# The gate's logits computed with the tokens stationary and the gate's weights moving

## The chip, the cores and the metric

The kernel runs on one core of a Trainium2 chip. The core has a matrix engine (TensorE; PE in the profile, with its weight loads shown apart as PEld), VectorE (DVE), ScalarE (ACT), GpSimd (POOL) and the DMA queues, which SyncE (SP) starts. The metric is the device time of one execution in microseconds (us), as the median of several runs.

A matrix multiplication on TensorE is a pair of instructions. A weight load (LDWEIGHTS) puts the *stationary* operand into the array, at most 128 columns of it, and a MATMUL then streams the *moving* operand past it. The output has the stationary operand's columns on its partitions and the moving operand's columns along its rows.

## What is computed

Three stages follow one another: an attention with packed keys, a dense layer with a clipped activation, and a mixture of eight experts. The change is in the third stage's first line:

```python
logits = x @ w_gate                  # x: 2304 x 512, w_gate: 512 x 8
logits = logits - logits.max()
P = np.exp(logits)
for _ in range(8):
    P /= P.sum(1, keepdims=True) + 1e-09
    P /= P.sum(0, keepdims=True) + 1e-09
    P *= N / E
for e in range(E):                   # E = 8 experts
    h = np.maximum(x @ w1[e], 0.0)
    out += P[:, e:e + 1] * (h @ w2[e])
```

## The kernel before

The 2304 tokens are cut into six blocks of 384. While the dense layer is computed, its result `x` is summed in `acc[blk]`, one tile for a block: the 512 features lie on 128 partitions in four chunks (KC = 4), and the block's 384 tokens lie along the rows. The dense layer's first product is `layer1a` (lines 871 to 873 of the code), its second `layer2a` (lines 908 to 910), whose result VectorE adds into `acc` (line 929). Each of these products is made of three MATMULs, since numbers are split into a high and a low part. The expert stage does the same with `layer1b` (lines 982 to 984) and `layer2b` (lines 1040 to 1042); `operands` (from line 941) prepares what `layer1b` multiplies.

`gate(blk)` makes the logits of one block, and there are six such calls. Before the change a gate has four steps:

1. Line 1100: four matmuls, one for each chunk of 128 features. The chunk of `wg` is stationary, padded from 8 to 32 columns with zeros, and the chunk of 384 tokens moves. Each writes another 32 of the 128 output partitions (a column tile), so the four lie side by side in the array, and what comes out are four partial sums. The operands are plain float32, and the profile shows two pairs of instructions for one such matmul.
2. `copy` (line 297 on ScalarE, 298 on VectorE): the 128x384 partial sums go from PSUM to a tile `tmp`.
3. Line 1110: three transposes of 128x128 put the tokens on the partitions.
4. Line 1117: VectorE adds the four partial sums and writes 24 numbers on each partition into `L`.

When `L` is whole, `routing()` finds the largest logit and does the eight rounds of normalizing, on VectorE, with two small matmuls for the maximum (lines 1131 and 1140) and one in each round for the sum over the tokens (line 1170: a 128x128 tile of ones is stationary, 8 columns move).

The order of the instructions is made by a planner in the kernel (`Order.run`): every step has an engine, a cost in us that the author wrote down, a priority and the tiles it needs, and the planner puts next whatever can start first by these costs. So an edit to one step's cost or tiles can change the order of its neighbours on every engine. The planner only sets the order; on the chip each engine takes its instructions in that order and waits where an operand isn't there. The gate has priority 41 and runs as soon as its block of `acc` is finished, among the products of the dense layer; its steps stand at 0.75 us and 0.36 us on TensorE in the plan.

Of the kernel before, what the change touches and what calls it, by code (L numbers as in the profile page):

```python
# [12 lines left out]
ALU = mybir.AluOpType  # L13
AX = mybir.AxisListType
# [119 lines left out]
def t_dve(n, fast=False):  # L134
    return 0.065 + n / (1920.0 if fast else 960.0)


def t_act(n, psum=False):
    return (0.05 if psum else 0.095) + n / 1200.0
# [11 lines left out]
def tile_kernel(  # L151
# [16 lines left out]
    nc = tc.nc  # L168
# [4 lines left out]
    E, _, F2 = moe2_w1.shape  # L173
    KC = DM // 128
# [5 lines left out]
    TB = 384  # L180
# [7 lines left out]
    def pool(name, stack=ctx, **kw):  # L188
        return stack.enter_context(tc.tile_pool(name=name, bufs=1, **kw))

    const, dp, accp, hp, wp = (pool(n) for n in ("const", "dp", "accp", "hp", "wp"))
    ph = pool("ph", space=PSUM)
# [7 lines left out]
    def place(tag, where, count, late=0):  # L200

        res[tag] = Res(count)
        res[tag].pool, res[tag].first, res[tag].late = where, count, late
# [49 lines left out]
    ident = const.tile([128, 128], F32, name="ident")  # L253
# [17 lines left out]
    def hold(tag, shape, dt=F32):  # L271
        return Hold(res[tag], maker(tag, shape, dt, ("",)))
# [5 lines left out]
    def pe(cost, fn, **kw):  # L278
        return order.op([("PE", cost, fn)], **kw)

    def dve(cost, fn, **kw):
        return order.op([("DVE", cost, fn)], **kw)
# [4 lines left out]
    def gps(cost, fn, **kw):  # L287
        return order.op([("POOL", cost, fn)], **kw)
# [4 lines left out]
    def copy(dst, src, n, **kw):  # L293

        return order.op(
            [
                ("ACT", t_act(n, True), lambda: nc.scalar.activation(dst(), src(), AF.Copy)),  # L297
                ("DVE", t_dve(n), lambda: nc.vector.tensor_copy(dst(), src()), EASE),
            ],
            **kw,  # L300
        )
# [88 lines left out]
    def whole(g, which, prio, tag, early=False):  # L390

        _, w1, w2, f0 = groups[g]
        if which == "w1":
            src = w1[:, f0:f0 + FG].rearrange("(c p) f -> p c f", p=128)
        else:
            src = w2[f0:f0 + FG, :].rearrange("(c p) d -> p c d", p=128)
        wide = src.dtype == I64
        shape = list(src.shape)
        w = hold(tag, shape) if which == "w1" else pair(tag, shape)
        per = shape[1] // (2 if wide else 1)  # L400
        for i in range(0, shape[1], per):
            r = raw_piece(src[:, i:i + per, :], prio, turn_of("raw", early))

            def at(t, i=i, c0=0, n=per * shape[2]):
                return t[:, i:i + per, :].rearrange("p c n -> p (c n)")[:, c0:c0 + n]

            if wide:
                n = DEC_EARLY if early else DEC
                for c0 in range(0, per * shape[2], n):
                    split_f64(  # L410
                        r, c0, n, w, lambda t, at=at, c0=c0, n=n: at(t, c0=c0, n=n), prio, which == "w2",
                        "m_early" if early else "m",
                    )
            else:
                split_part(at, lambda r=r: r.t, w, per * shape[2], [r], prio)
        return w
# [396 lines left out]
    acc = [hold(f"acc{j}", [128, KC, TB]) for j in range(NB)]  # L813
# [3 lines left out]
    def psum(tag):  # L817
        return hold(tag, [128, 512])

    def tmp():  # L820
        return hold("tmp", [128, TB])
# [261 lines left out]
    def once(name, shape, dt=F32):  # L1083
        if name not in res:
            place(name, None, 0, 1)
        return hold(name, shape, dt)

    Pr = once("Pr", [128, NTT, E])
    L = once("L", [128, NTT * E])
    wg = once("wg", [128, KC, 32])  # L1090

    def gate(blk):
        c0 = blocks[blk][0] // 128
        nt = TB // 128
        kw = dict(prio=41)
        ps, lg = psum("ph"), tmp()

        def mm():
            for c in range(KC):
                nc.tensor.matmul(  # L1100
                    ps.t[32 * c:32 * c + 32, :TB], wg.t[:, c, :], acc[blk].t[:, c, :], start=True, stop=True
                )

        pe(0.75, mm, reads=[acc[blk], wg], writes=[ps], **kw)
        copy(lambda: lg.t, lambda: ps.t[:, :TB], TB, reads=[ps], writes=[lg], **kw)
        pt = psum("ph")

        def trans():
            for t in range(nt):
                nc.tensor.transpose(  # L1110
                    pt.t[:, t * 128:(t + 1) * 128], lg.t[:, t * 128:(t + 1) * 128], ident
                )

        pe(0.12 * nt, trans, reads=[lg], writes=[pt], **kw)
        dve(
            t_dve(nt * E * KC),
            lambda: nc.vector.tensor_reduce(
                L.t[:, c0 * E:(c0 + nt) * E].rearrange("p (t e) -> p t e", e=E),
                pt.t[:, :nt * 128].rearrange("p (t c e) -> p t e c", t=nt, c=KC)[:, :, :E, :],
                AX.X, ALU.add,  # L1120
            ),
            reads=[pt], fills=[L], **kw,
        )

    def routing():
# [68 lines left out]
    def early(gg):  # L1194

        return (9.4, 9.4, 13.4, 14.4, 100, 100, 100, 100)[gg]

    with tc.manual_schedule():
        nc.vector.memset(ones, 1.0)
        nc.vector.memset(three, 3.0)  # L1200
        nc.vector.memset(maskb, 0.0)
        nc.vector.memset(maskb[0:64, 0, :], 1.0)
        nc.vector.memset(maskb[64:128, 1, :], 1.0)
        nc.vector.memset(maskz, 0.0)
        for g in range(2):
            for h in range(2):
                r0 = 64 * g + 32 * h
                nc.vector.memset(maskz[r0:r0 + 32, g, h, :], 1.0)

        place("p0", att, 1)  # L1210
        place("p1", att, 1)
        p_sb = hold("p0", [128, 1, D]), hold("p1", [128, NU - 1, D])
        for u in range(NU):
            attention(u, p_sb)
        ws, pws = {}, {}

        def weights(gg):
            prio, soon = early(gg), gg < 4
            ws[gg] = (
                whole(gg, "w1", prio, "w1f", soon),  # L1220
                whole(gg, "w2", prio + 0.5, ("w2", "w2o")[gg % 2], soon),
            )

        for gg in range(4):
            weights(gg)
        order.op([("", 0.0, second_phase)], after=order.all)

        gps(0.2, lambda: nc.gpsimd.memset(wg.t, 0.0), writes=[wg], prio=90)
        dma(
            16,  # L1230
            lambda: nc.sync.dma_start(wg.t[:, :, :E], moe2_w_gate.rearrange("(c p) e -> p c e", p=128)),
            writes=[wg], prio=90,
        )
        begun = len(order.all)
        for i, (b, g, half) in enumerate(units):
            for gg in (2 * g, 2 * g + 1):
                if gg not in ws:
                    weights(gg)
                if (b, gg) not in pws:
                    pws[b, gg] = packed_weights(i, b, ws[gg][0])  # L1240
            hs = [pair("hs", [128, NFC, TB]) for _ in range(2)]
            for f in range(2 * NFC):
                layer1a(i, b, half, f, pws[b, 2 * g + f // NFC], hs[f // NFC])
            layer2a(i, g, b, half, [ws[2 * g][1], ws[2 * g + 1][1]], hs)
        uses = [[o for o in order.all[begun:] if a2[b] in o.holds] for b in range(B)]
        freed = []
        for b, count in enumerate((1, 2, 1, 2)):
            freed = [order.op([("", 0.0, first_operands(count))], after=[*uses[b], *freed])]
        order.op([("", 0.0, third_phase)], after=order.all[begun:])
        for blk in range(NB):  # L1250
            gate(blk)
        ops = {0: operands(0, 40)}
        routing()
        i = len(units)
        turn, done = 100 + G1, []
        for ps in passes:
            for pr in ps:
                if pr not in ops:
                    ops[pr] = operands(pr, 45 if pr > 1 else 200, [done[-1] if pr > 1 else done[6]])
            for g in range(G1, len(groups)):  # L1260
                wa, wb = combined(g, turn)
                w2 = whole(g, "w2", turn, "w2")
                turn += 1
                for pr in ps:
                    hs = [pair("hs", [128, NFC, TB]) for _ in range(2)]
                    done.append(layer1b(i, ops[pr], wa, wb, hs))
                    for h in range(2):
                        layer2b(i, g, 2 * pr + h, w2, hs[h])
                    i += 1
        order.run()  # L1270
# [32 lines left out]
```

## Time and profile before

| | |
|---|---|
| three runs | 1964.9, 1965.55 and 1965.96 us; median 1965.55 us |
| the profiled execution's own time | 1963.38 us |
| its span, first to last instruction | 1961.6 us |
| TensorE busy | 1918.5 us, 98% of the span |
| VectorE, ScalarE, GpSimd busy | 62%, 50%, 46% |
| share of TensorE in the chain that ended last | 87% |
| mean granted TensorE clock | 0.996 |

The profile shows one execution. A line of the timeline gives the start, the length, the engine, the code's line, output and inputs, and in brackets how long the engine had stood idle and for whom. MATMULs overlap: a new one starts before the listed end of the last, so what an instruction costs TensorE is read from start to start, and the listed ends are modelled. The granted clock is 1.00 at 2.4 GHz and 0.50 at 1.2 GHz.

### The profile page before, as it was taken

The numbers are of one execution on the slowest core, as the hardware profiler recorded it, in microseconds if no ns is written. First come the engines' busy times: TensorE is split into PE (matmuls) and PEld (weight loads), VectorE is DVE, ScalarE is ACT, GpSimd is POOL, SyncE is SP. The second block draws the span as 40 slices with busy tenths as digits, with TensorE's granted clock in tenths as the row PEclk, the third lists the DMA queues.
The fourth block names the chain that finished last, engine by engine and source line by source line (L and its number), as shares of the span: only waits on it lengthen the run. The fifth ranks groups of instructions, "written<-read, shape, count | busy, mean of one in ns | idle before, by whom it ended". The sixth has DMA issues, their size and how long they took to land.

```text
span 1961.6 us, 29114 instructions
## 1 busy us (share of the span) xinstructions
PE 1918.5 (98%) x10957; PEld 1733.8 (88%) x10957; DVE 1213.5 (62%) x2110; ACT 981.4 (50%) x2273; POOL 897.4 (46%) x961
## 2 busy tenths in 40 slices
PE   6899999999999999999999999999999999999998
PEld 4789989988989999999889999999999999999997
DVE  6886687446876666666736655555555555555554
ACT  6885775445465555554553444434444343444432
POOL 2454576346665555555633434334243333434321
PEclk9999999999999999999999999999999999999999
DMA  9920121001212222222311101011110110101002
GB/s 211 202 79 27 53 68 50 12 1 44 65 54 76 65 66 74 65 65 75 87 33 33 33 33 44 22 43 33 33 44 22 44 33 33 42 24 44 29 15 65
DMA packets 103549, 104.92 MB, mean 53 GB/s; under 512 B 42736, under 2 KB 78576, under 8 KB 103408
## 3 DMA queue, kind: packets, MB, share of 16 engines
q1 hardware_dynamic: 103408, 103.06, 19.2%
q8 instruction: 86, 1.41, 0.3%
q14 instruction: 55, 0.45, 0.1%
HBM read 98.32 MB, written 4.72 MB: 53 GB/s over the span
## 4 chain that ended last, share of the span: by engine, by line
PE 87%; DVE 5%; ACT 2%; POOL 2%; DMA 2%; issue 1%; SPq 0%; POOLq 0%; ACTq 0%; DVEq 0%
PE po L1042 13%; PE po L1040 13%; PE po L1041 13%; PE ph L982 12%; PE ph L984 12%; PE ph L983 12%; PE po L908 2%; PE po L909 2%; PE po L910 2%; PE ph L871 1%; POOL m L341 1%; DMA raw<-in_moe_w_out_dram 1%; PE ph L873 1%; PE ph L872 1%; PE ph L833 1%
## 5 line engine op out<-in xcount | busy, mean ns | idle before, releaser
L426 POOL TENSOR_TENSOR hsl<-tmp,hsh 128x384 fp32r<-128x384 f32 (+1 forms) x418 | 402.8, 975 | 815.9 <-PE ph L984 483.6
L1064 DVE SCALAR_TENSOR_TENSOR acc<-po,Pr,acc 128x512 f32<-128x512 f32 x504 | 372.8, 747 | 288.0 <-PE po L1042 286.5
L1042 PE MATMUL po<-w2h,hsl 128*128 128x512 f32 x1152 | 449.0, 390 | 0.4 <-DVE hsl L426 0.4
L1040 PE MATMUL po<-w2h,hsh 128*128 128x512 f32 x1152 | 449.1, 390 | 0.0
L1041 PE MATMUL po<-w2l,hsh 128*128 128x512 f32 x1152 | 449.0, 390 | 0.0
L297 ACT ACTIVATE tmp<-ph 128x384 f32<-128x384 f32 x291 | 141.2, 485 | 411.9 <-PE ph L984 405.6
L996 DVE TENSOR_TENSOR tmp<-ph,tmp 128x384 f32<-128x384 f32 x288 | 159.1, 552 | 267.1 <-PE ph L984 189.4
L1042 PEld LDWEIGHTS po<-w2h,hsl 128*128 128x128 f32 x1152 | 216.3, 188 | 45.8 <-DVE hsl L426 0.8
L1040 PEld LDWEIGHTS po<-w2h,hsh 128*128 128x128 f32 x1152 | 216.5, 188 | 41.5
L1041 PEld LDWEIGHTS po<-w2l,hsh 128*128 128x128 f32 x1152 | 216.4, 188 | 41.3
L421 ACT ACTIVATE hsh<-tmp 128x384 fp32r<-128x384 f32 (+1 forms) x512 | 245.5, 498 | 13.1 <-DVE tmp L886 8.9
L421 ACT ACTIVATE w2h<-raw 128x1024 fp32r<-128x1024 f32 x64 | 68.0, 1063 | 326.5 <-PE po L1042 318.1
L982 PE MATMUL ph<-ax,w1h 128*128 128x384 f32 x512 | 173.1, 338 | 0.6 <-ACT tmp L297 0.6
L983 PE MATMUL ph<-ax,w1h 128*128 128x384 f32 x512 | 172.6, 337 | 0.0
L984 PE MATMUL ph<-ax,w1l 128*128 128x384 f32 x512 | 172.5, 337 | 0.0
L1004 ACT ACTIVATE tmp<-tmp 128x384 f32<-128x384 f32 x288 | 149.7, 520 | 31.2 <-DVE tmp L996 24.8
L426 POOL TENSOR_TENSOR w1l<-raw,w1h 128x256 fp32r<-128x256 f32 (+1 forms) x123 | 155.8, 1267 | 0.0
L982 PE MATMUL ph<-xyh,w1xh 128*128 128x384 f32 x320 | 108.4, 339 | 0.1
L984 PE MATMUL ph<-xyh,w1xl 128*128 128x384 f32 x320 | 108.0, 337 | 0.0
L983 PE MATMUL ph<-xyl,w1xh 128*128 128x384 f32 x320 | 107.8, 337 | 0.0
L881 ACT ACTIVATE tmp<-ph,three 128x288 f32<-128x288 f32 x128 | 63.1, 495 | 85.1 <-PE ph L873 84.1
L426 POOL TENSOR_TENSOR w1xl<-m,w1xh 128x256 fp32r<-128x256 f32 x130 | 105.1, 827 | 0.2
(206 smaller groups left out, 4038.7 us busy)
## 6 DMA issues: line engine op xcount, KB each, us to landing
raw<-in_moe_w_dram SPq DMA_DIRECT2D x128, 512.0 KB, 3.6
raw<-in_moe_w_in_dram SPq DMA_DIRECT2D x16, 512.0 KB, 3.9
raw<-in_moe_w_out_dram SPq DMA_DIRECT2D x16, 512.0 KB, 3.8
k<-in_k_dram SPq DMA_DIRECT2D x32, 144.0 KB, 5.7
q<-in_q_dram SPq DMA_DIRECT2D x32, 144.0 KB, 4.8
v<-in_v_dram SPq DMA_DIRECT2D x8, 576.0 KB, 6.8
out_dram<-acc SPq DMA_DIRECT2D x36, 128.0 KB, 2.3
p<-in_p_dram SPq DMA_DIRECT2D x1, 224.0 KB, 5.5
```

The lines of the kernel that those rows point to most:

```text
L297: ("ACT", t_act(n, True), lambda: nc.scalar.activation(dst(), src(), AF.Copy)),
L421: t_act(n), lambda: nc.scalar.activation(dst(w.t[0]), src(), AF.Copy),
L426: lambda e: e.tensor_tensor(dst(w.t[1]), src(), as_f32(dst(w.t[0])), ALU.subtract),
L982: nc.tensor.matmul(out, wh[:, at + c, :], bh[:, c, :], start=first and c == 0, **on)
L983: nc.tensor.matmul(out, wh[:, at + c, :], bl[:, c, :], start=False, **on)
L984: nc.tensor.matmul(out, wl[:, at + c, :], bh[:, c, :], start=False, **on)
L996: t_dve(n), lambda: nc.vector.tensor_tensor(u.t, ps.t[:, :n], u.t, ALU.add),
L1004: t_act(n, bool(ps)), lambda: nc.scalar.activation(c.t, src(), AF.Relu),
L1040: nc.tensor.matmul(ps.t, hh[:, f, ts], wh[:, f, :], start=(f == 0), stop=False)
L1041: nc.tensor.matmul(ps.t, hh[:, f, ts], wl[:, f, :], start=False, stop=False)
L1042: nc.tensor.matmul(ps.t, hl[:, f, ts], wh[:, f, :], start=False, stop=(f == NFC - 1))
L1064: lambda row=row, share=share, ps=ps: nc.vector.scalar_tensor_tensor(row(), ps.t, share(), row(), ALU.mult, ALU.add),
```

## The change

The two operands of the gate's matmuls change places. A block's tokens are now stationary, 128 tokens at a time, and the eight columns of the gate's weights move past them. A block has three groups of 128 tokens and four chunks of features, so there are twelve matmuls where four were, and the chunks are summed in PSUM (`start` on the first, `stop` on the last). The result has the tokens on the partitions already. ScalarE's copy, the three transposes and VectorE's sum over the four parts go; VectorE copies 24 numbers on each partition into `L`. `wg` is no longer padded, and GpSimd's memset of it goes. The gate's one step on TensorE stands at 1.6 us in the plan.

```diff
-    wg = once("wg", [128, KC, 32])
+    wg = once("wg", [128, KC, E])
...
-        kw = dict(prio=41)
-        ps, lg = psum("ph"), tmp()
+        ps = psum("ph")
 
         def mm():
-            for c in range(KC):
-                nc.tensor.matmul(
-                    ps.t[32 * c:32 * c + 32, :TB], wg.t[:, c, :], acc[blk].t[:, c, :], start=True, stop=True
-                )
-
-        pe(0.75, mm, reads=[acc[blk], wg], writes=[ps], **kw)
-        copy(lambda: lg.t, lambda: ps.t[:, :TB], TB, reads=[ps], writes=[lg], **kw)
-        pt = psum("ph")
-
-        def trans():
             for t in range(nt):
-                nc.tensor.transpose(
-                    pt.t[:, t * 128:(t + 1) * 128], lg.t[:, t * 128:(t + 1) * 128], ident
-                )
-
-        pe(0.12 * nt, trans, reads=[lg], writes=[pt], **kw)
+                for c in range(KC):
+                    nc.tensor.matmul(
+                        ps.t[:, t * E:(t + 1) * E], acc[blk].t[:, c, t * 128:(t + 1) * 128], wg.t[:, c, :],
+                        start=(c == 0), stop=(c == KC - 1),
+                    )
+
+        pe(1.6, mm, reads=[acc[blk], wg], writes=[ps], prio=41)
         dve(
-            t_dve(nt * E * KC),
-            lambda: nc.vector.tensor_reduce(
-                L.t[:, c0 * E:(c0 + nt) * E].rearrange("p (t e) -> p t e", e=E),
-                pt.t[:, :nt * 128].rearrange("p (t c e) -> p t e c", t=nt, c=KC)[:, :, :E, :],
-                AX.X, ALU.add,
-            ),
-            reads=[pt], fills=[L], **kw,
+            t_dve(nt * E),
+            lambda: nc.vector.tensor_copy(L.t[:, c0 * E:(c0 + nt) * E], ps.t[:, :nt * E]),
+            reads=[ps], fills=[L], prio=41,
         )
...
-        gps(0.2, lambda: nc.gpsimd.memset(wg.t, 0.0), writes=[wg], prio=90)
         dma(
             16,
-            lambda: nc.sync.dma_start(wg.t[:, :, :E], moe2_w_gate.rearrange("(c p) e -> p c e", p=128)),
+            lambda: nc.sync.dma_start(wg.t, moe2_w_gate.rearrange("(c p) e -> p c e", p=128)),
             writes=[wg], prio=90,
         )
```

The planner's order around it moves too. On TensorE at the first gate, where `layer1a` (lines 871 to 873) runs on both sides of it, the order before is (a line has the code's line, the operation, output and inputs, the output's size, and a count; the numbers count tiles):

```order
L873 MATMUL ph_5345<-ax_94,pwl_5146 128x288
L1100 MATMUL ph_5356<-acc_0_1253,wg_2229 32x384 x4
L871 MATMUL ph_5366<-ax_94,pwh_5145 128x288
L872 MATMUL ph_5366<-ax_94,pwh_5145 128x288
L873 MATMUL ph_5366<-ax_94,pwl_5146 128x288
L871 MATMUL ph_5366<-ax_94,pwh_5145 128x288
L872 MATMUL ph_5366<-ax_94,pwh_5145 128x288
L873 MATMUL ph_5366<-ax_94,pwl_5146 128x288
L1110 MATMUL ph_5376<-ident,tmp_5373 128x128 x3
```

and now, on the same engine at the same place:

```order
L873 MATMUL ph_5344<-ax_94,pwl_5145 128x288
L1100 MATMUL ph_5355<-wg_2229,acc_0_1253 128x8 x12
L871 MATMUL ph_5374<-ax_94,pwh_5144 128x288
L872 MATMUL ph_5374<-ax_94,pwh_5144 128x288
L873 MATMUL ph_5374<-ax_94,pwl_5145 128x288
L871 MATMUL ph_5374<-ax_94,pwh_5144 128x288
L872 MATMUL ph_5374<-ax_94,pwh_5144 128x288
L873 MATMUL ph_5374<-ax_94,pwl_5145 128x288
```

The gate is one piece in the same place, and the three transposes behind the next six MATMULs are gone; the other five gates change in the same way.

On VectorE, at the last gate and the entry of the routing (`w2l` and `w1l` are the low parts of the experts' weights; line 996 adds parts of `layer1b`; lines 1129 and 1134 take the maximum, 1143 copies it), the order before is:

```order
L959 TENSOR_TENSOR tmp_6147<-acc_0_1253,acc_0_1607 128x384
L426 TENSOR_TENSOR w2l_6141<-raw_4614,w2h_6140 128x1024
L1117 TENSOR_REDUCE L_5392<-ph_6184 128x24
L1129 TENSOR_REDUCE mx_6199<-L_5392 128x1
L996 TENSOR_TENSOR tmp_6160<-ph_6190,tmp_6160 128x384
L426 TENSOR_TENSOR w1l_6210<-raw_5128,w1h_6209 128x512
L996 TENSOR_TENSOR tmp_6182<-ph_6201,tmp_6182 128x384
L1134 TENSOR_REDUCE mm_6229<-ph_6216 1x1
L996 TENSOR_TENSOR tmp_6085<-ph_6190,tmp_6085 128x384
L1143 COPY nm_6259<-ph_6248 128x1
```

and now (lines 1108, 1116, 1121 and 1130 are the copy into `L`, the two maxima and the copy of the maximum):

```order
L959 TENSOR_TENSOR tmp_6165<-acc_0_1253,acc_0_1607 128x384
L426 TENSOR_TENSOR w2l_6159<-raw_4613,w2h_6158 128x1024
L1108 COPY L_5382<-ph_6171 128x24
L1116 TENSOR_REDUCE mx_6200<-L_5382 128x1
L1121 TENSOR_REDUCE mm_6213<-ph_6202 1x1
L996 TENSOR_TENSOR tmp_6106<-ph_6204,tmp_6106 128x384
L1130 COPY nm_6230<-ph_6216 128x1
L426 TENSOR_TENSOR w1l_6228<-raw_5127,w1h_6227 128x512
```

The three steps that lead to the maximum stand closer together: one addition of line 996 is left between them, where three and a split of weights stood. On TensorE the two small matmuls of the maximum come that much earlier too: six MATMULs of `layer1b` lie between the last gate and the first of them, and six between the first and the second.

## Rows read from the trace of the kernel before

**Rows 1.** The page: busy time of each engine, and the last chain's shares.

```profile
PE 1918.5 (98%) x10957; PEld 1733.8 (88%) x10957; DVE 1213.5 (62%) x2110; ACT 981.4 (50%) x2273; POOL 897.4 (46%) x961
PE 87%; DVE 5%; ACT 2%; POOL 2%; DMA 2%; issue 1%; SPq 0%; POOLq 0%; ACTq 0%; DVEq 0%
```

**Rows 2.** Stretches: PE, PEld, DVE, ACT, POOL busy; PE clock, DMA share, GB/s.

```profile
130.00:380.00 250.00, 244.35 (x1795) 225.10 (x1793) 166.86 (x378) 153.24 (x400) 139.60 (x174) 1.00 0.16 47
380.00:465.00 85.00, 83.98 (x619) 76.54 (x618) 38.59 (x93) 37.22 (x85) 37.73 (x42) 1.00 0.03 7
```

**Rows 3.** Timeline at the first gate: start us, length us, engine, line, operation.

```profile
388.00 0.29 PE L873 MATMUL ph<-ax,pwl 128*128 128x288 f32 x1
388.22 0.16 PEld L1100 LDWEIGHTS ph<-acc,wg 128*32 128x32 f32 x8 [0.16 <-DVE acc L929]
...
389.24 0.29 PE L872 MATMUL ph<-ax,pwh 128*128 128x288 f32 x1
...
389.28 0.49 ACT L297 ACTIVATE tmp<-ph 128x384 f32<-128x384 f32 x1 [0.39 <-PE ph L1100]
...
389.77 0.30 PE L873 MATMUL ph<-ax,pwl 128*128 128x288 f32 x1
...
389.90 0.49 PE L1110 MATMUL ph<-ident,tmp 128*128 128x128 f32 x3
...
390.36 0.29 PE L872 MATMUL ph<-ax,pwh 128*128 128x288 f32 x1
```

**Rows 4.** Line 1100 of all gates: what its weight loads waited for, us, times.

```profile
  DVE acc L929: 0.8, 5
```

**Rows 5.** Line 1170, the routing's sum over tokens: weight loads, ns min/median/max.

```profile
L1170 PEld LDWEIGHTS ph<-cs,ones x16: 186/188/192, 471.2 to 511.6; 128*128 128x128 f32 x16
```

**Rows 6.** Timeline of TensorE at one such sum: MATMULs.

```profile
475.24 0.34 PE L984 MATMUL ph<-ax,w1xl 128*128 128x384 f32 x1
475.42 0.29 PE L1170 MATMUL ph<-cs,ones 128*128 128x8 f32 x2
475.56 0.42 PE L982 MATMUL ph<-xyh,w1xh 128*128 128x384 f32 x1
475.81 0.34 PE L983 MATMUL ph<-xyl,w1xh 128*128 128x384 f32 x1
475.99 0.34 PE L984 MATMUL ph<-xyh,w1xl 128*128 128x384 f32 x1
```

**Rows 7.** The same place: weight loads.

```profile
475.24 0.36 PEld L1170 LDWEIGHTS ph<-cs,ones 128*128 128x128 f32 x2
475.53 0.19 PEld L982 LDWEIGHTS ph<-xyh,w1xh 128*128 128x128 f32 x1
475.64 0.19 PEld L983 LDWEIGHTS ph<-xyl,w1xh 128*128 128x128 f32 x1
```

**Rows 8.** Timeline of the weight loads in the attention, 64 columns wide.

```profile
64.15 1.13 PEld L733 LDWEIGHTS tp<-ppT,qT 128*64 128x64 f32 x36 [0.56 <-ACT ppT L297]
```

**Rows 9.** Timeline of VectorE at the last gate.

```profile
458.75 2.04 DVE L426 TENSOR_TENSOR w2l<-raw,w2h 128x1024 fp32r<-128x1024 f32 x1
462.35 0.26 DVE L1117 TENSOR_REDUCE L<-ph 128x24 f32<-128x96 f32 x1 [1.56 <-PE ph L1110]
```

**Rows 10.** Timeline of TensorE behind its two longest waits of the expert stage.

```profile
578.47 0.69 PE L982 MATMUL ph<-ax,w1xh 128*128 128x384 f32 x1 [3.65 <-DVE tmp L996]
970.08 0.69 PE L982 MATMUL ph<-xyh,w1h 128*128 128x384 f32 x1 [2.37 <-ACT tmp L297]
```

**Rows 11.** Stretches of 1 us behind the second of them (columns as in Rows 2).

```profile
970.00:971.00 1.00, 0.92 (x3) 0.92 (x4) 1.00 (x2) 0.82 (x3) 0.90 (x2) 0.50 0.36 78
976.00:977.00 1.00, 1.00 (x6) 1.00 (x5) 1.00 (x1) 0.20 (x1) 1.00 (x2) 0.60 0.51 145
```

**Rows 12.** Waits of TensorE, 280 to 300 us: total us, times, longest.

```profile
PE ph L833 <- DVE tmp L886: 2.2, 1, 2.2
```

**Rows 13.** Timeline of VectorE ahead of the first of the two long waits.

```profile
563.90 0.75 DVE L1064 SCALAR_TENSOR_TENSOR acc<-po,Pr,acc 128x512 f32<-128x512 f32 x1 [1.55 <-PE po L1042]
```

## The prediction, made before the changed kernel ran

> **What bounds the kernel now.** I read the page first: TensorE is busy for 98% of the span and makes up 87% of the chain that ended last [rows 1]. Then the stretch in which the six gates lie, 380 to 465 us: TensorE is busy for 83.98 of 85 us there, VectorE, ScalarE and GpSimd for less than half [rows 2]. So at the gates time is what TensorE spends, from start to start, and work taken off the other three is worth nothing by itself. The timeline at one gate says what TensorE spends now [rows 3], and one at a sum of the routing shows the form of instruction that the change brings in: a plain float32 weight load of 128 columns with 8 moving columns behind it [rows 5 to 7].
>
> **What goes.** Around the first gate an ordinary pair of `layer1a` takes 0.1325 us (from 389.24 to 389.77 there are four pairs) [rows 3]. From the L873 ahead of the gate to the L872 behind it there are 1.24 us; two ordinary pairs would be 0.265, so the gate's four matmuls cost 0.975. From the L873 ahead of the transposes to the L872 behind them there are 0.59 us, so these cost 0.59 - 0.265 = 0.325. Together 1.30 us, six times: 7.8 us, all on the path. ScalarE's copy of 0.49 us [rows 3] and VectorE's sum of 0.26 us [rows 9] go as well, but they lie beside TensorE's next products, on engines that are less than half busy [rows 2]; only the transposes waited for the copy, and six MATMULs stood between. GpSimd's memset and the padding lie hundreds of us ahead of their use. I set all of that at zero. If the cover were not there, the most that could be gained is the copy and the sum themselves, 0.75 us for a gate.
>
> **What comes.** Twelve matmuls for each gate. A plain float32 matmul is two pairs (the old gate's four matmuls show eight loads [rows 3], and so does each sum in the routing: 16 loads for 8 sums [rows 5]). So there are 24 loads of 128 columns in a gate, 144 in all, each with only eight moving columns to hide under. What is such a pair worth? At the sum in the routing the first load hides under L984. The next loads begin at 475.53 and 475.64, 0.11 us apart, although the listed length of one is 0.19 [rows 7]: loads follow one another at 0.11 us, and the eight columns vanish in that. The MATMULs say the same: from L984 to L983 there are 0.57 us; two pairs of 384 columns at 0.18 (the step from L983 to L984 behind it) would be 0.36, so the two small pairs cost some 0.1 us each [rows 6]. The three transposes, which also load 128 columns each, cost 0.325 / 3 = 0.108 [rows 3]. I take 0.11. The bounds, from both sides: 0.028 us, the pace of 36 loads of 64 columns in the attention, 1.13 us less the last one's own 0.14 [rows 8]; and 0.188, the listed length of a load, if none began before the last was done [rows 5].
>
> Two small things more. In five of the six gates the loads waited for VectorE's last addition to `acc` (0.8 us in all) [rows 4]; at the first gate they began at 388.22 where the next pair was due at 388.13, so 0.09 late [rows 3]. That stays. And the first load now reads `acc` itself and can't begin before that, so it lies bare: another 0.11.
>
> The gate after: 0.09 + 0.11 + 24 x 0.11 = 2.84 us. Before: 1.30. More by 1.54 us, six times **+9.2 us**.
>
> **The Trainium skill speaks against this change**: "TensorEngine Tiling (Array Packing)", section "Performance Considerations", advises for a moving side of 64 columns or less to swap the operands and to use column tiling. That is the form the kernel had, and the change goes the other way. The rows above agree: eight loads of 32 columns, all four column tiles, lie within 0.16 us [rows 3]; the sum doesn't need the rule.
>
> **What the planner moves.** In the first five gates the neighbours on TensorE stay. At the last one VectorE's long split (2.04 us from 458.75) stands ahead of the logits' step in both orders; it ends at 460.79, and VectorE then waited 1.56 us for the transposes [rows 9]. Those stood twelve MATMULs, 12 x 0.18 [rows 6], behind the old gate's matmuls, which so ended at about 462.35 - 0.33 - 2.16 = 459.9; the new gate ends 2.84 - 0.975 = 1.87 later, at 461.7, and the copy finds VectorE free. The first matmul of the maximum stands six MATMULs, about 1.05 us, behind the gate on TensorE; before it VectorE has the copy and one reduction of about 0.26 each [rows 9], 0.6 with the handing over. The second stands as far behind the first with one reduction between. Neither should be waited for; if each were by half a microsecond, that is +1. The order of `layer1b` and of the operands farther on is the same in both kernels, so the two long waits of TensorE, 3.65 and 2.37 us [rows 10], should stay: VectorE stood idle for 1.55 us waiting for TensorE just ahead of the first [rows 13], so it is paced by TensorE and shifts with it.
>
> The profiled execution took 1963.38 us, and its span 1961.6; by the sum it would be 1972.6. The median of the three runs is 2.2 us above that execution, and a difference carries over: 1965.55 + 9.2 = **1974.8 us**, 0.47% slower. A measurement of this kernel can tell about 0.2%, 3.9 us, from no change.
>
> **The rivals.**
>
> *Loads that hide.* If the loads of a gate ran at the pace of the attention's, 0.028 us [rows 8], a gate would take 0.2 + 24 x 0.028 = 0.87 us, less by 0.43 than now, and the kernel 1965.55 - 2.6 = 1963.0 us: not slower. It decides itself at a pair of 0.046 us, where the new gate costs as much as the old. For it: these loads follow very short streams at a fast pace. Against: they go in turn to two halves of the array and are half as wide, while the new ones take the whole; the rows of just the new form show 0.11. The Trainium skill, "TensorE: Matmul & The Clock Gate", section "What happens when you issue a matmul", has loads drawn ahead under the running matmul and a floor of about 25 ns for a matmul of up to 64 columns; an estimate by that floor alone is 24 x 0.025 = 0.6 us a gate, which would be this rival; the same section's price of a load, columns over 1.2, is 107 ns, and the trace agrees with that one.
>
> *The clock falls within the gate.* TensorE stood idle for 2.37 us, and the granted clock was 0.50 in the first microsecond behind it; it was still down at the start of the seventh (0.60 for 976 to 977) [rows 10, 11]. That is 6.8 us at half speed, 3.4 us lost. After a wait of 2.2 us between 280 and 300 us it stayed at 1.00 [rows 2, 12]. The new gate keeps TensorE for 2.8 us with loads and hardly any streaming; if that counts as idle, the clock could fall behind a gate. One fall gives 1978.2, all six 1995. Against: the loads go on without a gap, and no row shows loads alone for so long.
>
> *The fall at 970 us goes away.* A wait of 2.37 us lost the clock, one of 2.2 kept it [rows 10 to 12]; the changed kernel reaches the same wait at another moment, and it need not lose the clock again. Then 1974.8 - 3.4 = 1971.4.
>
> *The waits soak it up.* If what TensorE waits for at 575 and 968 us were paced by something other than TensorE, arriving 9.2 us later would use up both waits, 3.65 + 2.37, and with them a fall of the clock behind each, both taken at the 3.4 us of the second: 1974.8 - 12.8 = 1962.0, at the edge of faster. Against it stands VectorE's own idle time ahead of the first [rows 13].
>
> **How the numbers follow.** The forecast, loads at about 0.11 us and the clock as it was: 0.62. The clock falls at a gate: 0.14 (once 0.08, more often 0.06). The fall at 970 goes: 0.10. Loads that hide: 0.08. Waits that soak it up: 0.06. The range: the forecast, down to the fall that goes away with a margin (1970) and up to one fall more (1978.2), also the gate's loads at the pace of ordinary pairs, 0.1325, which gives 0.22 + 3.18 = 3.40 us a gate and 1978.2: **1970 to 1979**. Left out are the hidden loads, the waits that soak it up and several falls, 0.20. Slower by over 0.2%: 0.62 + 0.14 + 0.10, rounded down to 0.85. Within 0.2%: 0.11, most of the hidden loads and half of the soaking up. Faster: 0.04.
>
> **What would show it.** In the changed profile, line 1100 with 144 loads and 144 MATMULs, the loads about 0.11 us apart and 2.6 us for a gate's 24; about 2.84 us from the MATMUL ahead of the gate to the next, beyond an ordinary pair; no line 1110; TensorE's share still 98%; the clock 1.00 through the gates; the two waits of 3.65 and 2.37 us in their places, some 9 us later; no wait at lines 1118 and 1127. Loads 0.05 us apart or less, a clock below 1 between 385 and 480 us, or a long wait that is gone would prove me wrong, each at its own step.

## The result, and the profile after

The changed kernel takes 1986.51 us, the median of four runs from 1981.8 to 1991.28 us, against 1965.22 us for the kernel before, run in turn with it. The ratio is 1.0113, with a 95% interval from 1.0101 to 1.0125: slower by 22 us (20 to 25), where 9.2 were forecast. The profiled execution is the fastest of the four, 1981.8 us with a span of 1980.0, so 18.4 us of the 22 can be looked for in it.

From the page, the busy times and the chain that ended last, answering to [rows 1]:

```profile
PE 1937.1 (98%) x11035; PEld 1752.7 (89%) x11035; DVE 1214.9 (61%) x2116; ACT 980.0 (49%) x2268; POOL 890.9 (45%) x953
PE 87%; DVE 5%; ACT 3%; POOL 2%; DMA 2%; issue 1%; SPq 0%; POOLq 0%; ACTq 0%; DVEq 0%
```

TensorE is still the bound. Its busy time rose by 18.6 us, as much as the span (18.4): the time is spent in TensorE's own instructions, not in new waits.

The timeline at the first gate, to be laid beside [rows 3] (start, length, engine, line):

```profile
388.84 0.29 PE L873 MATMUL ph<-ax,pwl 128*128 128x288 f32 x1
388.84 2.78 PEld L1100 LDWEIGHTS ph<-wg,acc 128*128 128x128 f32 x24
388.97 2.74 PE L1100 MATMUL ph<-wg,acc 128*128 128x8 f32 x24
...
391.57 0.38 PE L871 MATMUL ph<-ax,pwh 128*128 128x288 f32 x1
391.75 0.18 DVE L1108 COPY L<-ph 128x24 f32<-128x24 f32 x1 [1.53 <-PE ph L1100]
391.79 0.30 PE L872 MATMUL ph<-ax,pwh 128*128 128x288 f32 x1
```

From the L873 ahead of the gate to the L872 behind it there are 2.95 us; less two ordinary pairs (0.265) the gate costs 2.69 us. With 1.30 before, that is 1.39 us more for a gate and 8.3 us for six. The whole difference is not there.

The rest comes in two parts. First, the clock. Stretches of the changed kernel; the column behind POOL's is TensorE's granted clock (columns as in [rows 2]):

```profile
380.00:455.00 75.00, 73.98 (x573) 71.15 (x573) 30.31 (x79) 25.78 (x60) 25.50 (x30) 1.00 0.00 1
455.00:458.00 3.00, 3.00 (x13) 3.00 (x14) 1.65 (x5) 1.32 (x3) 0.47 (x2) 0.54 0.00 0
459.00:472.00 13.00, 13.00 (x96) 13.00 (x95) 6.33 (x10) 5.43 (x12) 6.62 (x6) 1.00 0.01 1
473.00:475.00 2.00, 2.00 (x8) 1.82 (x6) 0.28 (x1) 1.57 (x4) 0.48 (x1) 0.50 0.62 240
```

The fifth gate ends at 455 us and the sixth at 471.6, and behind each the clock is at 0.50 for some 3 us. Before the change it was 1.00 there [rows 2]. TensorE had not stood idle: it had been at the gate's loads without a gap.

Second, the long expert stage. One stretch of 900 us in which TensorE never waits, first of the kernel before, then of the changed one; the number in brackets behind PE's busy time is the count of its MATMULs:

```profile
1000.00:1900.00 900.00, 900.00 (x4547) 818.09 (x4546) 503.58 (x734) 383.27 (x845) 336.68 (x350) 1.00 0.11 34
```

```profile
1000.00:1900.00 900.00, 900.00 (x4517) 815.95 (x4516) 496.57 (x728) 384.07 (x844) 336.14 (x350) 1.00 0.12 35
```

The same products in the same order, at a full clock and with no idle time, but 30 fewer of them in 900 us: 30/4547 of 900 is 5.9 us. The diff touches nothing there. When the MATMULs of the two traces are laid side by side, the changed kernel falls behind by 0.60% of the time everywhere from 600 us to the end, but for the two long waits. It is the 384-column products of `layer1b` that do most of it: between 1000 and 1900 us their starts are 173.4 ns apart before and 174.8 after on the mean. The 512-column products of `layer2b` lose about half as much, 227.0 to 227.8, and that in the first nine or so behind each block of `layer1b`.

What the diff does touch is where things lie. `wg` shrank from 512 to 128 bytes a partition, and in the compiled programs every tile placed behind it lies 384 bytes lower: four of the `tmp` tiles, `acc` of the last two blocks, `layer1b`'s weights (`w1`, `w1x`) and the routing's small tiles. `layer1b`'s weights began at 416 modulo 512 bytes and now begin at 32. So the theories to be told apart were: the addresses (A), or the gate and its order (B), for the expert stage; and for the clock, the long run of loads in a gate (C), or chance (D).

### The profile page after: what moved, and what is told of

Same layout as the page of the kernel before. It is cut to its first block, busy times and chain, and to the rows that moved or that the text cites. A ratio compares the mean times of both kernels' runs of the same rounds, so it can differ in the third digit from the quotient of the medians.

```text
span 1980.0 us, 29260 instructions
## 1 busy us (share of the span) xinstructions
PE 1937.1 (98%) x11035; PEld 1752.7 (89%) x11035; DVE 1214.9 (61%) x2116; ACT 980.0 (49%) x2268; POOL 890.9 (45%) x953
## 4 chain that ended last, share of the span: by engine, by line
PE 87%; DVE 5%; ACT 3%; POOL 2%; DMA 2%; issue 1%; SPq 0%; POOLq 0%; ACTq 0%; DVEq 0%
PE po L1042 13%; PE po L1041 13%; PE po L1040 13%; PE ph L982 12%; PE ph L984 12%; PE ph L983 12%; PE po L908 2%; PE po L909 2%; PE po L910 2%; PE ph L871 1%; POOL m L341 1%; PE ph L873 1%; PE ph L872 1%; PE ph L833 1%; DMA raw<-in_moe_w_out_dram 1%
## 5 line engine op out<-in xcount | busy, mean ns | idle before, releaser
L984 PE MATMUL ph<-ax,w1l 128*128 128x384 f32 x512 | 173.4, 339 | 0.0
L983 PE MATMUL ph<-ax,w1h 128*128 128x384 f32 x512 | 173.3, 338 | 0.0
L426 POOL TENSOR_TENSOR w1l<-raw,w1h 128x512 fp32r<-128x512 f32 (+1 forms) x122 | 153.9, 1262 | 0.0
```

The lines of the kernel that those rows point to most:

```text
L426: lambda e: e.tensor_tensor(dst(w.t[1]), src(), as_f32(dst(w.t[0])), ALU.subtract),
L983: nc.tensor.matmul(out, wh[:, at + c, :], bl[:, c, :], start=False, **on)
L984: nc.tensor.matmul(out, wl[:, at + c, :], bh[:, c, :], start=False, **on)
```

## The experiments

Each was run beside the kernel before, five runs where an interval is given (four for the gate twice); ratios are to the kernel before. None of these kernels leaves out part of the computation.

**The new gate, old addresses.** The tile of weights is padded to 32 columns again; all else is as changed.

```diff
-    wg = once("wg", [128, KC, E])
+    wg = once("wg", [128, KC, 32])
...
-                        ps.t[:, t * E:(t + 1) * E], acc[blk].t[:, c, t * 128:(t + 1) * 128], wg.t[:, c, :],
+                        ps.t[:, t * E:(t + 1) * E], acc[blk].t[:, c, t * 128:(t + 1) * 128], wg.t[:, c, :E],
...
-            lambda: nc.sync.dma_start(wg.t, moe2_w_gate.rearrange("(c p) e -> p c e", p=128)),
+            lambda: nc.sync.dma_start(wg.t[:, :, :E], moe2_w_gate.rearrange("(c p) e -> p c e", p=128)),
```

> The changed kernel with its new gate, but with the tile of the gate's weights padded to 32 columns again (only the first 8 are loaded and used), so that every tile in the on-chip memory lies where it lay before the change. The order on every engine is that of the changed kernel. Theory A, the addresses cost time: the step from one 384-column product of layer1b to the next falls back from 174.8 to 173.4 ns, and the time falls by the 8 to 9 us that had been lost in the expert stage, from 1986.5 to about 1978. Theory B, the new gate or the new order itself slows the expert stage: the step stays 174.8 ns and the time about 1986.

Measured: 1977.69 us, ratio 1.0079 [1.0067, 1.0092], against 1.0113 for the changed kernel: 0.34%, 6.7 us, came back with 384 bytes of padding. The same stretch as above:

```profile
1000.00:1900.00 900.00, 900.00 (x4546) 817.82 (x4546) 497.60 (x729) 386.39 (x850) 335.70 (x350) 1.00 0.11 35
```

One MATMUL fewer than before the change. Laid beside the kernel before, MATMUL by MATMUL, the padded kernel loses nothing in the expert stage: it is 13.84 us behind at 1013 us and 13.84 at 1950. The changed kernel goes from 12.74 to 18.37 us behind in that time, and from 11.78 to 13.93 between 602 and 960 us. Theory A holds, and B falls for this part.

**The old gate, new addresses.** The kernel before, with `wg` wider than it need be, so that what lies behind it moves up.

```diff
-    wg = once("wg", [128, KC, 32])
+    wg = once("wg", [128, KC, 72])
...
-                    ps.t[32 * c:32 * c + 32, :TB], wg.t[:, c, :], acc[blk].t[:, c, :], start=True, stop=True
+                    ps.t[32 * c:32 * c + 32, :TB], wg.t[:, c, :32], acc[blk].t[:, c, :], start=True, stop=True
```

> The kernel before, with its old gate, but the tile of the gate's weights 72 columns wide (the first 32 are used, all are set to zero), so that everything behind it lies 640 bytes higher: at the same place modulo 1024 bytes as in the changed kernel. Theory A, addresses: the step of the 384-column products rises from 173.4 to 174.8 ns and the time by 8 to 9 us, from 1965.2 to about 1974, with no change to any gate. Theory B: 173.4 ns and 1965.2 us, no change.

> The kernel before, with the tile of the gate's weights 40 columns wide: everything behind it lies 128 bytes higher, at the same place modulo 512 bytes as in the changed kernel, but 512 bytes off modulo 1024. Theory A with a period of 512 bytes or less: about 1974 us and 174.8 ns, as with 72 columns. Theory A with a longer period: 1965.2 to 1974, another step than with 72 columns. Theory B: 1965.2 us.

Measured: 1969.62 us, ratio 1.0038 [1.0025, 1.005] with 72 columns; 1971.9 us, 1.0045 [1.0032, 1.0059] with 40. The stretch, with 72 and then with 40 columns:

```profile
1000.00:1900.00 900.00, 900.00 (x4519) 816.47 (x4518) 496.74 (x729) 382.75 (x843) 335.90 (x349) 1.00 0.11 34
```

```profile
1000.00:1900.00 900.00, 900.00 (x4519) 816.48 (x4519) 496.80 (x730) 383.18 (x844) 335.73 (x348) 1.00 0.11 34
```

The loss appears in a kernel that has no new gate at all, 7 to 9 us of it, and it is the same for 640 and for 128 bytes, so the place modulo 512 decides here.

**Which tile.** In the first of two kernels an unused tile of 640 bytes ahead of `layer1b`'s weights moves these and the routing's tiles alone. In the second `wg` has 40 columns, which moves `tmp` and `acc`, and an unused tile of 384 bytes brings the weights to 512 bytes from their old place.

```diff
+            if tag == "w1" and i == 0:
+                pool.tile([128, 160], F32, tag="gap", name="gap")
             got = [pool.tile(shape, dt, tag=f"{tag}{x}_{i}", name=f"{tag}{x}_{i}") for x in parts]
```

> The kernel before with an unused tile of 640 bytes a partition ahead of layer1b's weights: these weights and the routing's small tiles behind them lie 640 bytes higher, the tiles tmp and acc where they were. If the stationary weights' address sets the step of the 384-column products: 1969.6 us as with everything shifted, and as few MATMULs between 1000 and 1900 us (4519 where before had 4547). If it is the address of what VectorE and ScalarE write (tmp, acc): 1962.6 us and some 4547.

> The counterpart: the kernel before with tmp and acc shifted by 128 bytes (the gate's weights 40 columns wide) and an unused tile that moves layer1b's weights on to 512 bytes from their old place, so at the same place modulo 512. If the weights' address decides: some 4547 MATMULs between 1000 and 1900 us, as before the change, and about 1962.6 us. If the address of tmp or acc decides: some 4519 and 1970 us.

Measured: 1971.49 us, ratio 1.0039 [1.0025, 1.0053], for the first; 1963.79 us for one run of the second, beside a median of 1963.47 for the kernel before. The stretch, of the first and of the second:

```profile
1000.00:1900.00 900.00, 900.00 (x4520) 816.48 (x4519) 497.26 (x730) 383.06 (x843) 334.54 (x348) 1.00 0.11 34
```

```profile
1000.00:1900.00 900.00, 900.00 (x4547) 818.00 (x4546) 503.70 (x734) 383.66 (x844) 336.75 (x350) 1.00 0.11 34
```

Moving the weights costs all of it, moving `tmp` and `acc` nothing. The routing's tiles moved along with the weights in every kernel here, and one of them, `Pr`, is read by VectorE in the expert stage. But the loss isn't tied to what the other engines do at the moment. In the changed trace the steps inside a block of `layer1b` repeat, from the fourth on, the same five values: 177.5, 174.2, 173.3, 177.5 and 170.8 ns on the mean of the 58 blocks between 1000 and 1900 us, with a spread of about 0.5 ns. In the kernel before they lie between 172.9 and 173.7 behind the first six. It is the place of the stationary operand of `layer1b`.

**Which places.** The kernel before with 34, 38, 48 and 56 columns in `wg`, one run each.

> The kernel before with the tile of the gate's weights 34 columns wide: everything behind it lies 32 bytes higher, layer1b's weights at 448 modulo 512 in place of 416. If only the changed kernel's place (32 modulo 512) is bad: some 4547 MATMULs between 1000 and 1900 us and about 1963 us. If the place of before (416) is one of few good ones: some 4520 and 1970 us.

> The same with 38 columns: 96 bytes higher, layer1b's weights at 0 modulo 512, so that the 512 bytes of one load lie within one block of 512. If only 32 modulo 512 is bad: 4547 MATMULs between 1000 and 1900 us and 1963 us. If 416 is one of few good ones: 4520 and 1970 us. A count above 4547 would mean a place better than that of before.

> The same with 48 columns: 256 bytes higher, layer1b's weights at 160 modulo 512. If only 32 modulo 512 is bad: 4547 MATMULs between 1000 and 1900 us and 1963 us. If 416 is one of few good ones: 4520 and 1970 us.

> The same with 56 columns: 384 bytes higher, layer1b's weights at 288 modulo 512. If only 32 modulo 512 is bad: 4547 MATMULs between 1000 and 1900 us and 1963 us. If 416 is one of few good ones: 4520 and 1970 us.

Measured, beside one run of the kernel before at 1965.96: 1978.79, 1965.04, 1965.18 and 1971.32 us. The stretch, in that order:

```profile
1000.00:1900.00 900.00, 900.00 (x4496) 817.18 (x4496) 491.86 (x725) 379.04 (x833) 331.33 (x345) 1.00 0.11 34
```

```profile
1000.00:1900.00 900.00, 900.00 (x4542) 817.77 (x4542) 503.56 (x733) 383.60 (x843) 337.40 (x350) 1.00 0.11 34
```

```profile
1000.00:1900.00 900.00, 900.00 (x4546) 817.68 (x4545) 501.96 (x733) 383.79 (x844) 336.63 (x350) 1.00 0.11 34
```

```profile
1000.00:1900.00 900.00, 900.00 (x4520) 816.38 (x4519) 497.02 (x729) 382.83 (x843) 335.97 (x349) 1.00 0.11 34
```

Both theories written for these four were too simple: 160 and 0 modulo 512 are as good as 416, or nearly; 288 is as bad as 32; 448 is worse than either (51 MATMULs fewer, 10 us of the 900). 416 and 160 are the same place modulo 256, and so are 32 and 288. No place beat that of before.

**The gate in pieces.** The new gate with the padded tile, its twelve matmuls in three steps with some ten products of the layers between; in a second kernel this is so for the last two blocks alone.

```diff
-        def mm():
-            for t in range(nt):
-                for c in range(KC):
...
-        pe(1.6, mm, reads=[acc[blk], wg], writes=[ps], prio=41)
+        last = []
+        for t in range(nt):
+            last = [pe(0.55, lambda t=t: mm(t), reads=[acc[blk], wg], fills=[ps], after=last, lat=1.0 * (t < nt - 1), prio=41)]
```

> The new gate with the padded tile (addresses as before the change), cut into three steps of four matmuls, one for each 128 tokens, with some ten products of the layers between them. Theory C, the long run of loads lets the clock fall: no clock below 1.00 between 385 and 480 us here, where the one-piece gate shows falls behind its fifth and sixth gate; two more bare first loads a gate cost 6 x 2 x 0.11 = 1.3 us, each fall that goes gives 1.7 us or more, so the time is 0 to 6 us below the padded one-piece gate and its runs lie closer together. Theory D, the falls have nothing to do with the gate's length: they stay, and the time is 1.3 us above the padded one-piece gate.

> As the padded one-piece gate, but only the last two gates, those behind which the trace showed the clock fall, are cut into three steps of four matmuls each. Theory C1, the falls behind these two gates are the whole difference between the one-piece gate (1977.7 us, clock 0.993) and the gate all in pieces (1971.9 us, clock 0.997): about 1971 us and 0.997, since only 2 x 2 bare loads are added (0.4 us). Theory C2, falls behind the first four gates in other executions have their share: between 1972 and 1978 us.

Measured: 1971.92 us, ratio 1.0049 [1.0036, 1.0061], with all gates in pieces; 1975.05 us, 1.0059 [1.0046, 1.0072], with the last two alone; 1.0079 was the padded gate in one piece. The stretch of the gates, in one piece, with the last two in pieces, and with all in pieces (the clock stands behind POOL's column):

```profile
385.00:510.00 125.00, 123.25 (x832) 116.60 (x832) 67.66 (x161) 50.16 (x111) 52.81 (x58) 0.97 0.05 18
```

```profile
385.00:510.00 125.00, 123.36 (x840) 117.07 (x839) 65.16 (x162) 51.53 (x114) 53.91 (x57) 0.99 0.07 22
```

```profile
385.00:510.00 125.00, 122.53 (x839) 115.42 (x838) 69.75 (x164) 53.43 (x118) 57.63 (x59) 1.00 0.08 22
```

With all gates in pieces no fall is left. With the last two in pieces one came behind the first gate instead, behind which neither the changed kernel nor the padded one showed any:

```profile
393.00:395.00 2.00, 2.00 (x11) 2.00 (x10) 0.45 (x1) 0.50 (x1) 0.00 (x0) 0.50 0.03 8
```

So the gate at which the clock falls differs from one execution to the next. Of the sixteen gates in one piece in the traces of the changed kernel, the padded one and this one it was five, the fifth and sixth twice and the first once; of the 24 pieces in the two kernels with pieces it was none. In the nine traces of kernels with the old gate there is no fall between 380 and 520 us. That is theory C, and of its two forms C2. The mean clocks of the runs say the same without a trace: 0.992 to 0.994 in the five runs in one piece, 0.993 to 0.996 with the last two in pieces, 0.997 to 0.998 with all in pieces, 0.995 to 0.998 in the runs of the kernel before beside them. The intervals of the two kernels with pieces overlap, so their times alone don't order them. The extra 1.3 us expected for bare first loads did not come. In the trace the first piece costs 0.90 us (1.17 from the L873 ahead of it to the L872 behind it, less 0.265), so three at this price cost 2.7 us, as one long gate does:

```profile
387.95 0.29 PE L873 MATMUL ph<-ax,pwl 128*128 128x288 f32 x1
388.08 0.96 PE L1099 MATMUL ph<-wg,acc 128*128 128x8 f32 x8
388.90 0.38 PE L871 MATMUL ph<-ax,pwh 128*128 128x288 f32 x1
389.12 0.30 PE L872 MATMUL ph<-ax,pwh 128*128 128x288 f32 x1
```

**The gate twice.** The padded gate in one piece, its matmuls issued two times in a row.

```diff
-            for t in range(nt):
+            for t in [0, 1, 2] * 2:
```

> As the padded one-piece gate, but the twelve matmuls of a gate are made twice in a row (48 loads in place of 24; the second pass writes the same sums again). The price of a load: at the forecast's 0.11 us 24 more of them cost 2.64 us a gate and 15.8 us in all, at the 187 ns listed 27 us, hidden nothing. Theory C, a longer run of loads lets the clock fall more: further falls behind the gates between 385 and 500 us, the mean clock below 0.993 and the time above 1977.7 + 15.8 = 1993.5 us by some 2 to 15 us. Theory D, the length of the run doesn't matter to the clock: 1993.5 us and 0.993.

Measured: 2007.85 us, ratio 1.0227 [1.0213, 1.0241], that is 29 us above the one-piece gate. The timeline at its fifth gate, and the stretches with the gates:

```profile
474.88 0.29 PE L873 MATMUL ph<-ax,pwl 128*128 128x288 f32 x1
475.01 5.42 PE L1100 MATMUL ph<-wg,acc 128*128 128x8 f32 x48
480.29 0.38 PE L871 MATMUL ph<-ax,pwh 128*128 128x288 f32 x1
480.50 0.37 PE L872 MATMUL ph<-ax,pwh 128*128 128x288 f32 x1
```

```profile
385.00:400.00 15.00, 15.00 (x99) 14.69 (x99) 3.17 (x10) 3.20 (x8) 1.30 (x2) 0.77 0.00 1
400.00:415.00 15.00, 15.00 (x114) 14.62 (x110) 4.81 (x14) 2.20 (x5) 2.65 (x4) 0.91 0.01 1
415.00:430.00 15.00, 15.00 (x102) 13.59 (x101) 6.26 (x11) 5.75 (x13) 5.43 (x6) 0.84 0.00 0
430.00:450.00 20.00, 20.00 (x121) 19.15 (x122) 5.36 (x12) 4.82 (x12) 3.69 (x5) 0.76 0.00 1
450.00:480.00 30.00, 28.98 (x223) 28.75 (x221) 8.15 (x25) 6.80 (x17) 8.03 (x10) 0.94 0.01 1
480.00:510.00 30.00, 30.00 (x175) 29.23 (x176) 14.09 (x27) 12.70 (x28) 11.36 (x12) 0.83 0.12 36
```

At this gate the clock stayed up until the loads were done, and 48 of them took 5.28 us, 0.110 each. Over the gate's whole place there are 5.62 - 0.265 = 5.36 us, 2.67 more than for 24 loads: 16 us for six gates, the price of the forecast. The other 13 us are the clock's: it is below 1 in every stretch with a gate, at 0.986 to 0.984 over the runs. Loads that go on for longer, still without a gap, bring it down more surely: in this trace it fell at all six gates, at five of them before the loads were done. Theory D falls.

## Why the prediction was wrong

The direction was right, but the 9.2 us of the forecast are less than half of the 22 measured, and 1986.5 lies above the range. Two steps failed: the padding, set at zero, moved other tiles and so cost some 7 to 8 us, and several falls of the clock at the gates, left out of the sum and the range, cost some 6. The sum in the end, from ratios and rows: the gates 8.3 us, the addresses 6.7 (with and without the padding in the changed kernel) to 7.7 (the weights alone moved), and 7.8 by the two traces laid side by side, the clock 5.9 (one piece against pieces, 1.0079 less 1.0049) to 7.2 (what is left of 0.79%, 15.5 us, behind the gates' 8.3). That makes 21 to 23 of the 22 us. The intervals of the ratios are some 2.5 us wide to either side, and the clock's two figures are of the padded kernel; for the changed one, 22 less 8.3 and 7.8 leaves 6.

- **What goes, 1.30 us a gate, and what comes, 2.84: right.** The gate costs 2.69. The 0.09 us of waiting for `acc` is gone (no wait stands ahead of line 1100 in the changed trace). The 24 loads take 2.60 us (388.97 to 391.57), where 2.64 was set, and the bare 0.11 came to 0.09, in the step behind the gate (391.57 to 391.79, where an ordinary one is 0.13). The term came out at 8.3 us where 9.2 were written. Rows of a like instruction, the routing's sum, had given the price of a load to the hundredth.
- **The copy, the sum and the memset at zero: right. The padding at zero: here the prediction failed.** It set both to zero since they lie hundreds of microseconds ahead of their use. That is true of the memset, but padding is bytes too, and taking it away moved 22 tiles, at a cost of 6.7 to 7.8 us. No rival spoke of it. Nothing in the profile of before shows it either, since all of its rows have the same addresses; only the allocation could have raised the question, and only a run could have priced it.
- **Loads that hide** is refuted: 0.110 us a load, 48 in a row. Of the two prices in the Trainium skill ("TensorE: Matmul & The Clock Gate", section "What happens when you issue a matmul"), that of a load, columns over 1.2, agrees with the trace; the floor of 25 ns for short streams isn't what binds here, where each has a load of 128 columns ahead of it. The advice of the Trainium skill against this change ("TensorEngine Tiling (Array Packing)", section "Performance Considerations") was borne out: 2.69 us a gate in place of 1.30.
- **The clock falls within the gate: this rival happened.** Its price per fall was taken from one fall of 6.8 us; the falls of the changed trace, by the clock that it records, last 3.4 us and cost 1.7 each, but there is more than one, and their number varies from run to run. The changed kernel's four runs lie 9.5 us apart, and the slowest has the lowest mean clock (0.991 at 1991.28 us, 0.996 at 1981.8); the four of before lie 1.4 apart. The reason given against it, that the loads go on without a gap, is no reason: the clock fell behind loads that had none. Its times were rightly put on top of the forecast (1978.2 us for one fall, 1995 for all six); the error was that reason, the chance of 0.14 that came of it, and a range that left several falls out.
- **The two long waits stay: right.** In the changed trace they are 2.91 us (3.65 before) and 2.35 (2.37), 12.7 and 13.9 us later, so 0.8 us of the two was soaked up and no more:

```profile
591.21 0.44 PE L982 MATMUL ph<-ax,w1xh 128*128 128x384 f32 x1 [2.91 <-DVE tmp L996]
...
984.02 0.48 PE L982 MATMUL ph<-xyh,w1h 128*128 128x384 f32 x1 [2.35 <-ACT tmp L297]
```

  The falls of the clock at them were shorter in this execution (3.4 us where the one before had 6.8). With the shorter wait that gave back some 3 us, about what the two falls at the gates cost (3.4). So the profiled execution hides most of the clock's part. It is 4.7 us below the median of the runs; its account is 8.3 for the gates, 7.8 for the addresses (602 us to the end), 0.8 that was there ahead of the first gate, and 1.5 that is left for the clock and the rest.
- **The fall at 970 us goes away: it didn't.** It was there at 984 us, and shorter. That a wait of 2.37 us lost the clock and one of 2.2 kept it was no rule: the wait of 2.2 us near 281 us is there in all fourteen traces, and the clock fell at it in eight.
- **The routing's entry: right.** No wait at the first maximum, 0.4 us of issue at the second, and VectorE's copy into `L` waits for the gate alone.

A rule that bears on the term that was missed: the Trainium skill, "SBUF — State Buffer", section "Who interferes with whom", knows a single cause of contention between engines, the port that VectorE and GpSimd share, and has TensorE wait on no other engine. It says nothing of a price for an operand's place, and going by it alone one would put the move at nothing. The runs decide: the place of `layer1b`'s weights alone costs 0.39%. Why the place counts is not settled; the addresses of what moves past these weights were the same in all these kernels (480 modulo 512 bytes), so the place of the one relative to the other was not told apart from the place itself.

No version here beats the kernel before. The best form of the new gate, padded and in pieces, is slower by 0.49%, which is the gates' own 8.3 us and about 1 more, within the interval.

## What to carry to other kernels

Count a changed tile size as a move of every tile behind it, and look at the count of MATMULs in a long stretch without waits: if it differs where the code doesn't, compare addresses before anything else, and undo the move with padding. A run of weight loads with hardly a column behind them can cost TensorE its clock afterwards, though it is busy throughout; cut it up among other products. When a rival would add to the forecast rather than replace it, let the range hold it.

## What was not expected of the hardware

- The step between 384-column products depends on the address of the stationary operand: 173.4 ns at 416 and 160 modulo 512 bytes, 173.6 at 0, 174.8 at 32 and 288, 176.7 at 448, at a full clock and with nothing waiting (one trace each at 0, 160, 288 and 448).
- The granted clock fell to 0.50 at gapless runs of 24 loads (2.7 us), at five of the sixteen in three traces, and inside or behind all six runs of 48.
- Three pieces of eight loads cost about as much TensorE time (2.7 us) as one run of 24, and in two traces no fall of the clock.
